# A fused attention and bilinear FFN kernel: regrouping the matmuls between batch 1's pairs, and a later kv for batch 2

The kernel runs on one core of one Trainium2 chip. The metric is device time in microseconds (us), the median of several executions. Engines in the profile: PE is TensorE (matmuls), PEld its weight loads, DVE is VectorE, ACT is ScalarE, POOL is GpSimd, SP issues transfers.

## The reference

```python
kv  = einsum('bhsd,bhse->bhde', k, v)            # 8 batches, 8 heads, 576 tokens, head size 64
out = einsum('bhsd,bhde->bhse', q, kv)
rms = sqrt(mean(out * out, axis=-1) + 1e-6)
x   = (out / rms * g_norm), heads side by side   # 4608 x 512
y   = ((x @ w_a) * (x @ w_b)) @ w_out            # 512 -> 1536 -> 512
```

## The kernel before

The FFN works in strips of 512 tokens. For each strip come the products with w_a and w_b for 12 slices of d_ff, and then four output groups of 128 tokens, each the sum of 12 products with w_out in one bank of PSUM, the memory that TensorE writes its sums to. One such product I call a unit. While strip 0's output groups run, the kernel also computes attention of batch 1, whose four pairs of heads are put between pieces of six units each. I call this part batch 1's stretch:

```python
A = Attn(1)
h1, h2 = range(0, FC // 2), range(FC // 2, FC)        # FC = 12
...
ffn_o(0, 0, X[0])                                     # output group 0, in bank 4
pieces = [(1, h1), (1, h2), (2, h1), (2, h2), (3, h1), (3, h2)]
for n, (g, fcs) in enumerate(pieces):
    halves[0] = n > 0          # from here a product is two matmuls of 64 columns
    o_mm(0, g, O, fcs)         # six units, all groups in bank O = 3
    if fcs is h2:
        o_out(0, g, O)         # copy the finished group out, and store it
    if 0 <= n - 2 < NP:        # NP = 4 pairs
        A.pss(n - 2, SS)       # sums of squares (PE), then rs (ACT)
        A.pst(n - 2, X[n % 2]) # xt = q kv * rs (DVE)
    if 0 <= n - 1 < NP:
        A.x(n - 1, X[(n - 1) % 2])    # q times kv (PE); X is banks 4,5 or 0,1
        A.psq(n - 1, X[(n - 1) % 2])  # its squares, sq (ACT)
    if n < NP:
        A.qtr(n, 2)            # transposes of q (PE), in bank 2
        A.kv1(n, 2)            # kv (PE), in the same bank
        A.kv_out(n, ...)       # kvb (ACT)
        A.qtr_out(n, 2)        # qT (DVE)
```

In the next strip a unit is another thing: one slice of d_ff with w_a and then with w_b. Batch 2's kv (40 matmuls, four pairs) stands there after unit `k0 = 5`, and its reader 1.5 units later, in the middle of unit 7. Numbers ending in .5 mean "between the w_a half and the w_b half of a unit". Batch 2's v comes in two loads, 512 KB and 64 KB; the second is "the last piece".

## Time and profile before

| | before |
|---|---|
| time, first three runs | 312.58 us (312.45 to 313.01) |
| span of the profiled run | 310.8 us |
| TensorE busy | 98% at granted clock 1.00 |
| waits of TensorE in batch 1's stretch | 0.58 us |
| wait in batch 2's kv | 0.24 us |

TensorE is nearly always busy and the ends of its matmuls are modelled, so its waits hardly show in the busy shares. They are read from the distances between starts, as the prediction does below. The lines themselves are shown there.

### The profile page before, as it was taken

How to read it: one execution, taken by the hardware profiler on the slowest of the kernel's cores; microseconds unless marked ns; L12 is line 12 of the kernel's file. 1: busy time of each engine (PE TensorE's matmuls, PEld its weight loads, DVE VectorE, ACT ScalarE, POOL GpSimd, SP SyncE). 2: the span in 40 equal slices, each digit the busy share in tenths (PEclk: the TensorE clock that was granted, in tenths of full speed). 3: DMA queues.
4: the chain of work that ended last, by engine and by line, in shares of the span. 5: the costliest groups of instructions: out<-in, count | busy, mean ns of one | idle time of the engine just before them, and what ended most of it. 6: DMA issues, size and time to landing. Idle time of an engine off the chain costs nothing.

```text
span 310.8 us, 6542 instructions
## 1 busy us (share of the span) xinstructions
PE 304.3 (98%) x2684; PEld 157.6 (51%) x2701; DVE 140.6 (45%) x235; ACT 117.0 (38%) x231; POOL 101.3 (33%) x123
## 2 busy tenths in 40 slices
PE   7899999999999999999999999999999999999996
PEld 3444476655555555555555555444444444444444
DVE  4544335458248603484386123752782143214321
ACT  3743255354255313551564034632651233123310
POOL 8954991093274630043646300221240000000000
PEclk9999999999999999999999999999999999999999
DMA  8999999999899999047998990073021200030002
GB/s 180 197 196 199 201 188 168 161 169 184 174 137 185 139 174 193 2 84 134 178 177 118 162 188 2 19 160 110 20 51 42 103 1 0 34 103 0 0 36 101
DMA packets 94403, 36.29 MB, mean 117 GB/s; under 512 B 64934, under 2 KB 89894, under 8 KB 94374
## 3 DMA queue, kind: packets, MB, share of 16 engines
q0 software_dynamic: 59120, 18.44, 56.6%
q1 hardware_dynamic: 34786, 16.93, 25.0%
q10 hardware_dynamic: 468, 0.51, 0.6%
q8 instruction: 21, 0.34, 0.5%
q14 instruction: 8, 0.07, 0.1%
HBM read 37.78 MB, written 12.98 MB: 163 GB/s over the span
## 4 chain that ended last, share of the span: by engine, by line
PE 79%; DMA 12%; POOL 7%; issue 1%; ACT 0%; POOLq 0%
PE P L161 77%; DMA wb_t<-in_moe_w_b_dram 6%; DMA vtl<-in_v_dram 4%; DMA wo_t<-in_moe_w_out_dram 2%; PE P L293 1%; PE P L178 1%; POOL vt L119 1%; POOL qt L119 1%; POOL qs L142 1%; POOL kt L119 1%; POOL wa_t L477 0%; POOL wb_t L477 0%; POOL wo_t L134 0%; POOL ktl L145 0%; POOL vtl L145 0%
## 5 line engine op out<-in xcount | busy, mean ns | idle before, releaser
L377 DVE TENSOR_TENSOR ab<-P,asb 128x512 bf16<-128x512 f32 x108 | 74.4, 691 | 103.2 <-PE P L161 99.9
L161 PE MATMUL P<-xt,wb_t 128*64 128x512 bf16 (+1 forms) x641 | 111.4, 379 | 0.2
L161 PE MATMUL P<-xt,wa_t 128*64 128x512 bf16 (+1 forms) x636 | 111.0, 379 | 0.6 <-issue 0.2
L373 ACT CAST asb<-P 128x512 bf16<-128x512 f32 x108 | 63.1, 586 | 89.6 <-PE P L161 89.5
L161 PE MATMUL P<-wo_t,ab 128*64 128x512 bf16 (+3 forms) x673 | 95.5, 371 | 0.3
L161 PEld LDWEIGHTS <-ab 128*64 128x64 bf16 (+1 forms) x678 | 47.5, 106 | 45.0
L161 PEld LDWEIGHTS <-wa_t 128*64 128x64 bf16 (+1 forms) x644 | 46.0, 106 | 46.2 <-issue 0.6
L161 PEld LDWEIGHTS <-wb_t 128*64 128x64 bf16 (+1 forms) x644 | 45.8, 106 | 45.8
L330 POOL TENSOR_TENSOR sqt<-rst,g_all 128x512 f32<-128x512 f32 (+1 forms) x24 | 25.0, 1046 | 83.0 <-ACT rst L323 83.0
L429 ACT COPY osb<-P 128x512 f32<-128x512 f32 x17 | 10.0, 586 | 70.2 <-PE P L161 60.2
L431 DVE COPY osb<-P 128x512 f32<-128x512 f32 x18 | 12.4, 691 | 44.9 <-PE P L161 40.4
L142 POOL DMA_DIRECT2D qs<-in_q_dram x12 | 19.8, 1654 | 0.7 <-issue 0.3
L314 DVE TENSOR_REDUCE sst<-sqt 128x8 f32<-128x512 f32 (+1 forms) x24 | 16.3, 680 | 1.7 <-ACT sqt L310 1.5
L339 DVE TENSOR_TENSOR qv<-P,sqt 128x512 bf16<-128x512 f32 x18 | 12.3, 681 | 0.0
L330 POOL TENSOR_TENSOR k_x<-rst,g_all 128x512 f32<-128x512 f32 x6 | 6.3, 1044 | 17.4 <-ACT rst L323 17.4
L323 ACT ACTIVATE rst<-sst,eps_t 128x8 f32<-128x8 f32 (+1 forms) x30 | 9.0, 300 | 7.2 <-DVE sst L314 7.0
L310 ACT ACTIVATE sqt<-P 128x512 f32<-128x512 f32 x18 | 10.5, 585 | 0.1
L243 DVE SCALAR_TENSOR_TENSOR xt<-P,g_col,rs 128x288 bf16<-128x288 f32 x16 | 7.5, 511 | 5.1 <-ACT rs L233 5.1
L134 POOL DMA_DIRECT2D wo_t<-in_moe_w_out_dram x12 | 6.4, 530 | 6.7 <-DMA wb_t<-in_moe_w_b_dram 3.2
L233 ACT ACTIVATE rs<-P,eps_t 128x576 f32<-128x576 f32 (+1 forms) x9 | 6.1, 689 | 3.7 <-PE P L161 3.4
L139 POOL COPY gate<-qT 1x1 bf16<-1x1 bf16 x5 | 0.9, 177 | 18.9 <-DVE kvs L618 14.0
L444 PE MATMUL P<-zeros 128*128 128x512 bf16 x16 | 5.8, 510 | 1.2 <-DVE eps_t L461 1.2
(72 smaller groups left out, 131.7 us busy)
## 6 DMA issues: line engine op xcount, KB each, us to landing
out_dram<-osb SPq DMA_DIRECT2D x23, 256.0 KB, 2.1
qs<-in_q_dram POOLq DMA_DIRECT2D x12, 288.0 KB, 7.5
ktl<-in_k_dram POOLq DMA_DIRECT2D x6, 512.0 KB, 9.6
vtl<-in_v_dram POOLq DMA_DIRECT2D x6, 512.0 KB, 12.2
out_dram<-osb SPq DMA_DIRECT2D x13, 128.0 KB, 2.4
wo_t<-in_moe_w_out_dram POOLq DMA_DIRECT2D x12, 128.0 KB, 6.0
wa_t<-in_moe_w_a_dram POOLq DMA_DIRECT2D x5, 256.0 KB, 8.9
wb_t<-in_moe_w_b_dram POOLq DMA_DIRECT2D x5, 256.0 KB, 9.5
```

What stands on the lines that cost most here:

```text
L119: nc.gpsimd.dma_start(out=t[:, hs, :, :], in_=src[b, hs].rearrange("h (t c) d -> t h c d", c=EC))
L142: nc.gpsimd.dma_start(out=d[:, hs, :], in_=q[b, hs].rearrange("h t d -> t h d"))
L161: nc.tensor.matmul(o[r], lhsT=lhsT[:, r], rhs=rhs, **kw)
L310: nc.scalar.activation(sqt[c % 3][r], self.by_head(c)[r], AF.Square)
L314: nc.vector.reduce_sum(sst[c % 3][r], sqt[c % 3][r].rearrange("t j p d -> t (j p) d"), axis=mybir.AxisListType.X,)
L323: nc.scalar.activation(rst[c % 3][r], sst[c % 3][r], AF.Abs_reciprocal_sqrt, bias=eps_t[r], scale=1.0 / D,)
L330: nc.gpsimd.tensor_mul(sqt[c % 3][r].rearrange("t j p d -> t (j p) d"), rst[c % 3][r].unsqueeze(2).to_broadcast([n, H, D]), g_all[r].unsqu ...
L339: nc.vector.tensor_mul(t[r].rearrange("t (p j) d -> t j p d", j=2), self.by_head(c)[r], sqt[c % 3][r])
L373: nc.scalar.copy(self.t, self.a)
L377: nc.vector.tensor_mul(abt[self.s % 2][self.fc], self.b, self.t)
L429: nc.scalar.copy(t, P[:, i, :])
L431: nc.vector.tensor_copy(t, P[:, i, :])
```

## The change

The intent: let group 1 finish early in its own bank (bank 1), so that group 2 can follow at once without waiting for the copy out. That frees the cut between pieces from the boundaries of groups, so that more units can stand in front of the first pairs, whose loads are late. Batch 2's kv also moves half a unit back, behind its load.

```diff
-    h1, h2 = range(0, FC // 2), range(FC // 2, FC)
...
-    pieces = [(1, h1), (1, h2), (2, h1), (2, h2), (3, h1), (3, h2)]
-    for n, (g, fcs) in enumerate(pieces):
+    cuts = (12, 20, 27, 33, 36, 42, 48)
+    for n, cut in enumerate(cuts[1:]):
         halves[0] = n > 0
-        o_mm(0, g, O, fcs)
-        if fcs is h2:
-            o_out(0, g, O)
+        for i in range(cuts[n], cut):
+            g, fc = divmod(i, FC)
+            bank = X[1] + 1 if g == 1 else O
+            o_mm(0, g, bank, (fc,))
+            if fc == FC - 1:
+                o_out(0, g, bank)
...
-        k0, x0 = {1: (5, 6.5), 2: (1, 2.5), ...
+        k0, x0 = {1: (5.5, 6.5), 2: (1, 2.5), ...
```

The pieces become 8, 7, 6, 3, 6, 6 units.

More of the change, by code (lines that the diff above doesn't have):

```diff
@@ L608, in slot @@
             xs = tuple(x0 + x for x in (0, 1.5, 2.5, 4, 5))
-        k0, x0 = {1: (5, 6.5), 2: (1, 2.5), 3: (4, 5.5), 4: (0, 0.5), 5: (4, 5.5), 6: (0, 0.5)}[s]
+        k0, x0 = {1: (5.5, 6.5), 2: (1, 2.5), 3: (4, 5.5), 4: (0, 0.5), 5: (4, 5.5), 6: (0, 0.5)}[s]
         if n == k0 and s in (1, 2, 3, 5):
```

## The prediction

> **What bounds the kernel now.** I read the page first: busy shares, then the chain that ended last.
>
> ```profile
> PE 304.3 (98%) x2684; PEld 157.6 (51%) x2701; DVE 140.6 (45%) x235; ACT 117.0 (38%) x231; POOL 101.3 (33%) x123
> ...
> PE 79%; DMA 12%; POOL 7%; issue 1%; ACT 0%; POOLq 0%
> ```
>
> TensorE is the bound: busy for 98% of the span at granted clock 1.00 in every slice, and the chain is its matmuls from 60 us to the end. Both kernels do the same matmuls; only their order changes, apart from two units that run 128 columns wide and no longer as two 64-column halves. So the change can only win or lose the short holes between TensorE's instructions. The ends of matmuls are modelled, so I read holes from the distance between starts. The timeline of TensorE, asked in narrow windows over batch 1's stretch (start, us, group), gives:
>
> ```profile
> 39.13 0.45 PE L202 MATMUL P<-ident,qt 96*64 96x96 bf16 x12
> 39.60 0.38 PE L178 MATMUL P<-vt,kt 96*64 96x64 bf16 x12
> ...
> 41.33 0.45 PE L202 MATMUL P<-ident,qt 96*64 96x96 bf16 x12
> 41.82 0.38 PE L178 MATMUL P<-vt,kt 96*64 96x64 bf16 x12
> ...
> 43.31 0.44 PE L161 MATMUL P<-sq,ones 128*64 128x288 bf16 x4
> 43.55 0.44 PE L161 MATMUL P<-qT,kvb 128*64 128x288 bf16 x4
> 43.80 0.45 PE L202 MATMUL P<-ident,qt 96*64 96x96 bf16 x12
> 44.05 0.38 PE L178 MATMUL P<-vt,kt 96*64 96x64 bf16 x12
> ...
> 45.54 0.44 PE L161 MATMUL P<-sq,ones 128*64 128x288 bf16 x4
> 45.92 0.44 PE L161 MATMUL P<-qT,kvb 128*64 128x288 bf16 x4
> 46.16 0.45 PE L202 MATMUL P<-ident,qt 96*64 96x96 bf16 x12
> 46.42 0.38 PE L178 MATMUL P<-vt,kt 96*64 96x64 bf16 x12
> ```
>
> These are, pair by pair, the transposes of q (L202), kv (L178), the sums of squares (sq,ones) and q times kv (qT,kvb). Without a wait, transposes to kv is 0.26 us (46.16 to 46.42), squares to q times kv 0.24 (43.31 to 43.55). So kv of pair 0 waited 0.47 - 0.26 = 0.21, kv of pair 1 waited 0.49 - 0.26 = 0.23, and q times kv of pair 2 waited 0.38 - 0.24 = 0.14: together 0.58 us. What released them: the v loads are issued at 34.24, 36.47, 38.37 and 40.59 us in the GpSimd timeline, and the view of tile vt, one window for each, gives 5.3, 5.3, 5.6 and 5.6 us to landing, so they land at 39.54, 41.8, 43.97 and 46.19. The first two are the two waits for kv: batch 1's loads come one pair every 2.2 us, and TensorE keeps pace with them. The third wait is another thing; ScalarE and VectorE in that window:
>
> ```profile
> 43.78 0.74 ACT L233 ACTIVATE rs<-P,eps_t 128x576 f32<-128x576 f32 x1 [1.01 <-PE P L161]
> 44.42 0.64 ACT L225 ACTIVATE sq<-P 128x576 bf16<-128x576 f32 x1
> 44.95 0.43 ACT L189 CAST kvb<-P 64x64 bf16<-64x64 f32 x2
> 44.56 0.94 DVE L243 SCALAR_TENSOR_TENSOR xt<-P,g_col,rs 128x288 bf16<-128x288 f32 x2 [1.30 <-ACT rs L233]
> 45.42 0.45 DVE L209 COPY qT<-P 128x576 bf16<-128x576 bf16 x1
> ```
>
> A chain of latencies: squares of pair 0 (43.31) -> rs (43.78) -> sq of pair 1 and the cast of kvb on ScalarE, two xt products on VectorE -> qT of pair 2 (45.42 to 45.87) -> q times kv of pair 2 at 45.92. The two branches end within 0.05 us of each other.
>
> The fourth hole is kv of batch 2, where the chain of waits leaves the loads and joins TensorE:
>
> ```profile
> 47.20 13.45 DMA vtl<-in_v_dram
> 60.65 0.04 issue
> 60.69 0.69 PE P L178 x32
> ```
>
> The timeline has all 40 of these matmuls starting at 60.32 and the next unit at 61.19, 0.87 us; the same 40 take 0.63 us in the chain of waits at 86.37. So 0.24 us is waited for the last piece of v.
>
> **What the Trainium skill says.** "Perfetto Trace Analysis", section "Tensor Engine Instruction (MATMUL, LD_WEIGHTS)": a matmul's reported start comes after its semaphores are satisfied, and its end is estimated. The trace agrees: the waits show as late starts while busy stays at 98%. "TensorEngine Tiling (Array Packing)", "Key Properties": changing the tiling mode drains the engine. The trace agrees: from the last 128-column unit at 38.82 (39.13 less 0.31, single starts) to the first transpose is 0.31 us against 0.216 from unit to unit, 0.09 more; both kernels have this once in this stretch. "PSUM — Partial Sum Buffer", "PSUM bank collisions raise a hardware error": two engines must not use one bank at once, hence group 2 may start in the bank of group 1 only after its copy out. That is why the change needs a second bank. The trace of before shows no wait of group 2 for the copy: kv of pair 1 starts at 41.82 and the first unit at 42.01, the usual 0.19.
>
> **The change, part by part.** A unit (one fc of an output group, two 64-column matmuls) is 0.216 us. Before, pieces of 6, 6, 6, 6, 6, 6 units stood between pairs; after, 8, 7, 6, 3, 6, 6. Instruction order on VectorE and ScalarE is unchanged (the two listings differ in line numbers alone), and GpSimd's loads do not depend on this, so the landings stay. Replaying with the distances above:
> - Group 0 starts at 35.15 and takes 12 x 0.216, to 37.74. Eight units (1.73) and the mode change (0.09): transposes at 39.56, kv of pair 0 at 39.82. It landed at 39.54: no wait. Against 39.60 before, +0.22 (two units, 0.43, less the wait of 0.21).
> - kv 0.19, seven units 1.51, q times kv 0.24, transposes 0.26: kv of pair 1 at 42.02, landed 41.8, no wait. +0.20.
> - kv 0.19, six units 1.29: squares of pair 0 at 43.50, +0.19 (43.31). q times kv 43.75, transposes 43.99, kv of pair 2 at 44.25 (landed 43.97).
> - kv 0.19, three units 0.65: TensorE could do the squares of pair 1 at 45.09. But sq of pair 1 hangs on rs of pair 0, and that on the squares of pair 0, which are 0.19 later: sq starts at 44.61, ends 45.25, squares at about 45.31. A wait of 0.22. Then q times kv of pair 2 could start at 45.55, but qT of pair 2 comes 0.19 later than before: 45.92 + 0.19 = 46.11. A wait of 0.56.
> - Transposes, then kv of pair 3 at 46.61 against 46.42: +0.19. Its load landed at 46.19 and is not waited for in either kernel.
> - From there 6 and 6 units as before, everything shifted alike. Group 3 returns to group 2's bank: that copy starts after qT at about 45.99, takes 0.68, done by 46.7, and TensorE comes at 46.80. No wait.
>
> So 0.44 us of waits for loads and 0.14 for the chain go, and 0.78 of waits for the same chain come: about +0.19 at the end of the stretch. The gain was eaten because the units moved forward were the ones that covered the chain.
> - kv of batch 2 half a unit later: half a unit is four pairs, 0.86 us. It starts at 60.32 + 0.19 + 0.86 = 61.4, and the last piece landed at 60.65. The wait of 0.24 goes. Its reader is one unit (1.73 us) on, and the cast takes 0.42: nothing new waits.
>
> Sum: +0.19 - 0.24 = -0.05 us. All after 61 us is TensorE back to back, so this reaches the end: 312.58 - 0.05 = 312.53, call it 312.5.
>
> **Rivals.** (1) All four holes vanish, as the intent must be: -0.58 - 0.24 = -0.8, 311.8 us. Against it: kv of pair 3 cannot start before its load at 46.19 plus about 0.06 (39.54 to 39.60), so at most 46.42 - 46.25 = 0.17 of the 0.58 can be won while the loads land as they do. With the second hole that is -0.4, 312.2, the best I can see. It would come about if the chain has slack that the trace hides. (2) The three-unit piece costs more: the squares of pair 1 come late, so rs, sq and qT of pair 3 queue up behind one another, and a second wait follows at q times kv of pair 3 or at group 3's bank. In my replay each has 0.1 to 0.3 us to spare; if both were lost, +0.3, 312.8. (3) kv in the middle of a unit delays ScalarE or VectorE there: both idle over 1 us before each unit's copy in the timeline, so I give it nothing.
>
> **Range and chances.** All of this is under 0.3% of the time, and three runs of before already differ by 0.56 us. I take 312.1 (rival 1's floor, and a little) to 312.95 (rival 2, and the scatter). Over 2% either way would be 6 us, ten times every hole together: 1% each.
>
> **What would show it.** In the profile after: kv of pairs 0 and 1 about 0.26 us after their transposes; over 0.5 us from squares to q times kv in pair 2 (0.8 expected, 0.38 before); kv of pair 3 near 46.6; 40 matmuls of batch 2's kv in 0.63 us from about 61.4. The prediction is wrong if kv of pair 3 starts before 46.4, if v's landings move by more than 0.2 us, or if a hole over 0.2 us stands after 47 us that before does not have.

## The result

| | before | after |
|---|---|---|
| median of six runs | 312.69 us (312.36 to 313.13) | 312.86 us (312.66 to 313.05) |
| ratio | | 1.0004, 95% interval 0.9992 to 1.0017 |
| span of the profiled run | 310.8 us | 311.1 us |
| group 0's first unit to the last copy, same profiles | 272.71 us | 272.68 us |

A ratio is the mean time of one kernel's fast runs over that of the other's of the same rounds, so it is not quite the ratio of the medians. The medians differ by 0.17 us, less than either scatters.

The last row is the measure that I use from here on: the distance from the start of group 0's first unit to the start of the last copy on ScalarE, both single starts in the trace. It leaves out the kernel's first 35 us, which neither the change nor any experiment touches and which scatter. From the first matmul to group 0 took 33.96 us in the profile of before, 34.32 in that of after, and 33.96 to 34.44 over all thirteen profiles. That scatter alone is larger than the effect sought.

The distance is not wholly free of those 35 us, since group 0's start moves against batch 1's loads. In before, before_2 and kv_only, which wait for these loads, v of pair 0 landed 38.37 to 38.40 us after the first matmul and the squares of pair 3 stood at 48.52 to 48.56, though group 0 started anywhere from 33.96 to 34.14. A kernel that waits for the loads thus makes good a later start of group 0, and its distance comes out shorter; the changed kernel does not (squares of pair 3 at 48.74 to 49.18 in the five profiles with its pieces and both banks).

The page of the changed kernel, busy shares and the chain that ended last:

```profile
PE 304.7 (98%) x2682; PEld 157.0 (50%) x2699; DVE 140.8 (45%) x235; ACT 117.3 (38%) x231; POOL 101.3 (33%) x123
...
PE 97%; ACT 1%; DVE 1%; issue 1%
```

The loads are gone from the chain (they were 12% of it before, and the issues on POOL 7%). That alone does not show that no load is waited for: cuts_only below has the same shares, and its kv waited 0.22 us for a load. The landings show it for this profile: v of pairs 0 to 3 landed at 4.02, 6.24, 8.46 and 10.65 us after group 0's first unit and kv started at 4.69, 6.89, 9.12 and 11.47. Of the 1% each of ACT and DVE, 0.75 and 0.93 us stand in batch 1's stretch, and most of the rest before group 0. The timeline of TensorE shows the stretch (start, us, group). To compare with before, subtract group 0's first unit: 35.51 us here, 35.15 before.

```profile
39.92 0.45 PE L202 MATMUL P<-ident,qt 96*64 96x96 bf16 x12
40.20 0.35 PE L178 MATMUL P<-vt,kt 96*64 96x64 bf16 x12
...
42.15 0.42 PE L202 MATMUL P<-ident,qt 96*64 96x96 bf16 x12
42.41 0.35 PE L178 MATMUL P<-vt,kt 96*64 96x64 bf16 x12
...
43.89 0.41 PE L161 MATMUL P<-sq,ones 128*64 128x288 bf16 x4
...
44.83 0.82 PE L161 MATMUL P<-wo_t,ab 128*64 128x512 bf16 x6
45.68 0.44 PE L161 MATMUL P<-sq,ones 128*64 128x288 bf16 x4
46.49 0.44 PE L161 MATMUL P<-qT,kvb 128*64 128x288 bf16 x4 [0.37 <-DVE qT L209]
46.73 0.45 PE L202 MATMUL P<-ident,qt 96*64 96x96 bf16 x12
46.99 0.38 PE L178 MATMUL P<-vt,kt 96*64 96x64 bf16 x12
```

The kv of pairs 0 and 1 now follow their transposes after 0.28 and 0.26 us (0.47 and 0.49 before): the waits for the loads are gone. The three units at 44.83 end at about 45.48, but the squares of pair 1 start at 45.68, a wait of 0.20. From there to q times kv of pair 2 is 0.81 us instead of 0.24, a wait of 0.57, and the profile names its releaser: the copy of qT on VectorE. ScalarE and VectorE of the changed kernel in that window:

```profile
44.34 0.74 ACT L233 ACTIVATE rs<-P,eps_t 128x576 f32<-128x576 f32 x1 [1.02 <-PE P L161]
44.98 0.64 ACT L225 ACTIVATE sq<-P 128x576 bf16<-128x576 f32 x1
45.52 0.43 ACT L189 CAST kvb<-P 64x64 bf16<-64x64 f32 x2
45.12 0.94 DVE L243 SCALAR_TENSOR_TENSOR xt<-P,g_col,rs 128x288 bf16<-128x288 f32 x2 [1.30 <-ACT rs L233]
45.98 0.46 DVE L209 COPY qT<-P 128x576 bf16<-128x576 bf16 x1
```

It is the same chain with the same lengths: from the squares of pair 0 to q times kv of pair 2 it is 46.49 - 43.89 = 2.60 us, and before 45.92 - 43.31 = 2.61. Only fewer units lie over it now. Batch 2's kv in the changed kernel:

```profile
61.75 0.82 PE L178 MATMUL P<-vtl,ktl 128*64 128x64 bf16 x40
62.38 0.60 PE L161 MATMUL P<-xt,wb_t 128*64 128x512 bf16 x3
```

The 40 matmuls take 0.63 us to the next unit, and took 0.87 before: that wait is gone.

### The profile page after: what moved, and what is told of

Its sections match the earlier page's. It is cut to its first block, busy times and chain, and to the rows that moved or that the text cites. A ratio compares the mean times of both kernels' runs of the same rounds, so it can differ in the third digit from the quotient of the medians.

```text
span 311.1 us, 6538 instructions
## 1 busy us (share of the span) xinstructions
PE 304.7 (98%) x2682; PEld 157.0 (50%) x2699; DVE 140.8 (45%) x235; ACT 117.3 (38%) x231; POOL 101.3 (33%) x123
## 4 chain that ended last, share of the span: by engine, by line
PE 97%; ACT 1%; DVE 1%; issue 1%
PE P L161 90%; PE P L444 2%; PE P L178 1%; PE P L293 1%; PE P L202 1%; PE P L216 0%; DVE xt L243 0%; ACT sq L225 0%; ACT rs L233 0%; PE P L501 0%; DVE qT L209 0%; PE P L505 0%; PE P L517 0%; DVE zeros L455 0%; ACT o_end L668 0%
## 5 line engine op out<-in xcount | busy, mean ns | idle before, releaser
L444 PE MATMUL P<-zeros 128*128 128x512 bf16 x16 | 6.7, 573 | 1.2 <-DVE eps_t L461 1.2
```

What stands on the lines that cost most here:

```text
L444: nc.tensor.matmul(P[:, i, 0:cols], lhsT=zeros[:, 0:128], rhs=zeros[:, 0:cols], start=True, stop=True)
```

## The experiments

Theory A is that of the prediction: the waits for loads go, the wait for the chain takes their place, and the later kv wins a wait back. Rivals are named run by run. The measure is the distance defined above: 272.71 us before, 272.68 after. Each distance is from one profile. cuts_2, before_2, after_2 and the three held runs were executed once; their granted clock was 0.998 to 1.00.

### kv_only: the second part of the change alone

```diff
-        k0, x0 = {1: (5, 6.5), ...
+        k0, x0 = {1: (5.5, 6.5), ...
```

> The kernel before with the second part of the change alone (kv of batch 2 half a unit later). Theory A (waits come back): batch 1's stretch is as before, kv of batch 2 starts 0.86 us later than before and its 40 matmuls take 0.63 us and not 0.87, so the distance from group 0's first unit to the last copy out of the kernel (272.72 us before, 272.68 after) is 272.48, 0.24 less than before; time 0.999 of before. Rival B (the second part is worth nothing, a later wait for the same landing takes its place): 272.7.

Measured: distance 272.36, kv at 25.92 us after group 0's first unit, its 40 matmuls in 0.63 us; time 312.52 us against 312.57, ratio 0.9996 (0.9983 to 1.0008), not told apart from before. The wait in batch 2's kv is gone and no later one replaces it. But this profile does not show that the move did it: the last piece landed at 24.69, and kv at its old place, 25.06, would not have waited either. after_2 below shows it. A further 0.11 is from the start of group 0: v of pair 0 landed at 4.30 and not 4.41 after it, so the stretch, which is bound by the loads, ended 0.11 earlier. The loads themselves had hardly moved (38.40 us after the first matmul, 38.37 before); group 0 had started 0.14 later.

### cuts_only and cuts_2: the first part alone, looked at twice

```diff
-        k0, x0 = {1: (5.5, 6.5), ...      # from the changed kernel
+        k0, x0 = {1: (5, 6.5), ...
```

> The changed kernel without its second part. Theory A: the stretch of batch 1 ends 0.2 us later than before (kv of pair 3 and all after it), and the wait of batch 2's kv for its last piece shrinks by just that, from 0.24 to about 0.05, as the landing stays: distance from group 0's first unit to the last copy 272.72 to 272.77, as before, time ratio 1.000. Rival B: the second part is worth nothing, so this equals the changed kernel, 272.68, with no wait in kv of batch 2. Rival C: the two parts add up, so 272.72 + 0.2 = 272.92.

Measured: distance 272.89, ratio 1.0002 (0.9990 to 1.0014). That is rival C's figure and not theory A's. The stretch did end 0.20 later than before (squares of pair 3 at 14.76 us, before 14.56), but the wait in kv stayed at 0.22 us, because the last piece of v landed 0.19 later too. I had taken the landing as fixed. So I looked at the same kernel again, and at before.

> The changed kernel without its second part, profiled once more. In the first look batch 2's kv still waited 0.22 us, as its last piece landed 0.19 later than in the profile of before. Theory A (scatter of the landing): kv of batch 2 starts again 25.36 us after group 0's first unit; it waits max(0, landing - 25.49 + 0.04) and the distance is 272.67 plus that wait. Rival B: again a landing near 25.7 and a distance of 272.89.

The timeline of the first look, then that of the second:

```profile
60.81 1.05 PE L178 MATMUL P<-vtl,ktl 128*64 128x64 bf16 x40
61.66 0.41 PE L161 MATMUL P<-xt,wa_t 128*64 128x512 bf16 x2
```

```profile
60.53 0.82 PE L178 MATMUL P<-vtl,ktl 128*64 128x64 bf16 x40
61.16 0.63 PE L161 MATMUL P<-xt,wa_t 128*64 128x512 bf16 x4
```

The 40 matmuls took 0.85 us in one look and 0.63 in the other, with no instruction changed: the landing was at 25.68 us after group 0's first unit and at 23.65. Without the wait the distance was 272.67, as theory A had it. Over the thirteen profiles this landing lies between 23.65 and 25.68. So the three figures told nothing about how the two parts combine, only where the piece landed: the parts add up when it lands late, and the second part is worth nothing when it lands early.

### before_2 and after_2: both kernels once more

> The kernel before, profiled once more, to see how far the landing of batch 2's last piece of v moves from run to run: 25.49 us after group 0's first unit in the first profile, 24.2 to 25.7 in the five others. Theory A (the landing scatters by itself, with no regard to the kernel): it may land anywhere from 24.2 to 25.7, and kv of batch 2 waits only where it lands after about 25.3; distance 272.45 to 272.8, the stretch of batch 1 alike. Rival B (an early kv makes the landing late): again at 25.4 or later, wait again 0.24.

The stretch repeated: squares of pair 3 at 14.42 us (14.56 in the first profile), the landing was 25.42, and kv waited 0.31. Here theory A and rival B cannot be told apart, but cuts_2 (an early kv, and the earliest landing of all) speaks against B, and so does after_2 below (a later kv, and a landing at 25.58). These two show that kv's place does not fix the landing. Whether it shifts the odds stays open: of four profiles with kv at the early place three had a landing at 25.42 to 25.68, of nine with the later kv only after_2. The distance was 272.87, larger than I had allowed, and a wait elsewhere did it.

> The changed kernel once more. It waits for no load between group 0 and the end, so the distance should repeat to 0.03 us, 272.68, wherever the last piece of v lands, while the start of group 0 after the first matmul may lie anywhere from 33.9 to 34.5 us.

The stretch repeated exactly (squares of pair 3 at 14.76 against 14.77), and batch 2's kv waited for nothing although the piece landed at 25.58, which an undelayed kv at 25.36 would have met. It is the one profile that shows the second part of the change at work. But the distance was 272.96 and not 272.68. The timeline of after_2 at the start of strip 2, then that of after:

```profile
81.69 1.25 PE L161 MATMUL P<-wo_t,ab 128*64 128x512 bf16 x10
83.03 0.84 PE L161 MATMUL P<-xt,wa_t 128*64 128x512 bf16 x6
```

```profile
82.00 1.25 PE L161 MATMUL P<-wo_t,ab 128*64 128x512 bf16 x10
83.07 0.81 PE L161 MATMUL P<-xt,wa_t 128*64 128x512 bf16 x6
```

Ten 64-column matmuls are five units, 1.08 us; strip 2's first unit comes after 1.07 in one and after 1.34 in the other. This unit reads x of batch 2, which a transfer transposes; the third of these landed 47.68 us after group 0 in after_2 and 46.64 in after, and the unit started at 47.81. It waited so in two of thirteen profiles, once for each kernel (0.26 and 0.20 us). So my claim that the changed kernel waits for no load up to the end was too strong: this wait is there now and then, for both.

### even_cuts: pieces of 7, 7, 5, 5, 6, 6

```diff
-    cuts = (12, 20, 27, 33, 36, 42, 48)
+    cuts = (12, 19, 26, 31, 36, 42, 48)
```

> The changed kernel with pieces of 7, 7, 5, 5, 6, 6 units and not 8, 7, 6, 3, 6, 6: the chain from the squares of pair 0 to q times kv of pair 2 starts earlier and has more units over it. Theory A: no wait at kv of pairs 0 and 1, about 0.16 at kv of pair 2, about 0.2 at q times kv of pair 2 (0.56 in the changed kernel), none at the squares of pair 1; kv of pair 3 lies against its load, about 0.17 earlier than in the kernel before; the distance from group 0's first unit to the last copy is 272.72 - 0.19 - 0.24 = 272.3, ratio 0.9986 of before. Rival B (what costs is not the chain but the second bank or the early group 2): no better than the changed kernel, 272.68.

Measured: distance 272.35 (272.3 expected), 312.44 us against 312.57, ratio 0.9994 (0.9982 to 1.0006). With five units over the chain and not three, squares of pair 1 to q times kv of pair 2 is 0.38 us and not 0.81, so 0.14 of wait; kv of pair 2 waited for its load, as expected. The second bank and the early group 2 are as in the changed kernel, so rival B falls.

### squares_early: the head of the chain three units earlier

```diff
         for i in range(cuts[n], cut):
+            if n == 2 and i == cuts[n] + 3:
+                A.pss(0, SS)
+                A.pst(0, X[0])
...
-        if 0 <= n - 2 < NP:
+        if 0 < n - 2 < NP:
```

> The changed kernel, pieces unchanged, with the squares of pair 0 and their products (pss and pst of pair 0) put three units earlier, in the middle of their piece. Theory A (the chain that starts at the squares of pair 0 holds q times kv of pair 2): the wait at the squares of pair 1 goes (0.2), that at q times kv of pair 2 shrinks from 0.56 to at most 0.4, kv of pair 3 comes 0.3 to 0.37 us earlier and lies against its load; distance from group 0's first unit to the last copy about 272.3. Rival B (the copy of qT of pair 2 waits for its own kv alone, three units are too few whatever the squares do): q times kv of pair 2 stays where it is, distance 272.68.

Measured: distance 272.30 (272.3 expected), 312.41 us, ratio 0.9994 (0.9982 to 1.0007). The timeline of TensorE in this kernel, from the squares of pair 0 to kv of pair 3 (group 0's first unit is at 35.64):

```profile
43.37 0.41 PE L161 MATMUL P<-sq,ones 128*64 128x288 bf16 x4
...
45.60 0.41 PE L161 MATMUL P<-sq,ones 128*64 128x288 bf16 x4
46.23 0.44 PE L161 MATMUL P<-qT,kvb 128*64 128x288 bf16 x4 [0.22 <-DVE qT L209]
46.73 0.38 PE L178 MATMUL P<-vt,kt 96*64 96x64 bf16 x12
```

No unit was moved, only the squares of pair 0 with what follows them (rs, xt). The wait at the squares of pair 1 went, squares to q times kv of pair 2 fell from 0.81 to 0.63, and kv of pair 3 came at 46.73 - 35.64 = 11.09 us after group 0 and not at 11.48. The chain that begins at the squares of pair 0 is thus shown to hold pair 2. It is not alone: the squares came 0.65 us earlier and q times kv of pair 2 only 0.38, and 0.39 of its wait stayed. In this profile sq of pair 1 waits 0.15 for TensorE and qT of pair 2 waits 0.18 for the cast of kvb, so a second chain (q times kv of pair 1, sq, kvb, qT) stands close behind, and rival B has that much right. kv of pair 3 did not lie against its load, as I had expected: that landed at 10.77.

### one_bank: the changed pieces without the second bank

```diff
-            bank = X[1] + 1 if g == 1 else O
+            bank = O
```

> The changed kernel with group 1 back in group 2's bank, pieces as changed. Group 2's first unit now follows group 1's last at once and must wait for the copy out of the bank. Theory A: about 0.25 from the last unit to the copy's start, 0.59 of the copy and 0.05, so a wait of about 0.85 us inside the second piece (0.22 would be the usual distance, so about 0.65 to 0.7 of hole); nothing later makes it good, since the stretch waits for no load: distance from group 0's first unit to the last copy 272.68 + 0.65 = 273.3 to 273.4, ratio 1.002. Rival B (the second bank is only a convenience, the wait is given back by the waits at pair 2): 272.7 to 272.9.

Measured: distance 273.54, 313.51 us against 312.54, ratio 1.003 (1.0013 to 1.0047): slower by 0.3%, clear of the scatter. The timeline of TensorE in this kernel:

```profile
40.31 0.81 PE L161 MATMUL P<-wo_t,ab 128*64 128x512 bf16 x6
41.80 0.84 PE L161 MATMUL P<-wo_t,ab 128*64 128x512 bf16 x6 [0.68 <-ACT osb L429]
```

Group 2's first unit waits for the copy out of group 1's bank, and q times kv of pair 0, three units behind it, comes 0.84 us later than in the changed kernel (7.23 and 6.39 after group 0). I had expected 0.65 to 0.7, having taken off the usual distance between units from a sum that did not contain it. Nothing later made it good. So the second bank is not a nicety: without it these pieces lose 0.84 us.

### held_before, held_after and held_bank: batch 1 without its loads

```diff
-                kk, vv, rows = kt[self.b], vt[self.b], [EP] * EC
+                kk, vv, rows = kt[0], vt[0], [EP] * EC       # batch 0's k and v, long there
...
-                        qt[self.b][:, 2 * p + j, c, :],
+                        qt[0][:, 2 * max(p, 1) + j, c, :],   # and its q; k and v likewise
```

Batch 1's result is wrong. Its loads still run, so the transfers are as they were.

> Pieces as in the kernel before, batch 2's kv half a unit later, and batch 1 computed from batch 0's q, k and v that are already there (pairs 1, 1, 2, 3; a wrong result on purpose for batch 1), so that nothing in the stretch hangs on batch 1's loads, which still run. Theory A (the waits at kv of pairs 0 and 1 are the loads): both go, all after them comes 0.44 us earlier; the wait of about 0.14 at q times kv of pair 2 stays, since it is the chain. Distance from group 0's first unit to the last copy 272.71 - 0.44 - 0.24 = 272.03, or 272.1 if the kv of batch 2 now meets its landing. Rival B (those two waits are the return of bank 2 or the tiling mode, not the loads): 272.4 as in the run with batch 2's kv alone.

Measured: 272.20, where theory A said 272.03 to 272.1 and rival B 272.4. The waits at kv of pairs 0 and 1 went, but 0.16 us came up that I had not foreseen.

> The same edit on the changed kernel. Theory A: the changed kernel waits for no load in this stretch, only for the chain, so nothing moves: q times kv of pair 2 at 10.97 us after group 0's first unit, distance 272.68. Rival B (its pairs also hang on loads): earlier by what the loads cost, up to 0.4.

Measured: 272.67, and q times kv of pair 2 at 10.97: not moved by 0.01 us. The changed kernel's stretch hangs on no load.

> Pieces of six as in the kernel before, batch 2's kv later, batch 1 computed from batch 0's loads (wrong on purpose), and group 1 in its own bank. In the same kernel without the bank (held_before, 272.20) the first unit of group 2 came 0.35 us after kv of pair 1 and not 0.19. Theory A (with the loads gone the next wait is group 2's, for the copy out of group 1's bank): that 0.16 goes, distance 272.04. Rival B (something else stood there): 272.2.

Measured: 272.03 (272.04 expected). This kernel is held_before with group 1 in its own bank. The two timelines, held_before first:

```profile
41.56 0.35 PE L179 MATMUL P<-vt,kt 96*64 96x64 bf16 x12
41.91 0.41 PE L161 MATMUL P<-wo_t,ab 128*64 128x512 bf16 x2
```

```profile
41.69 0.35 PE L179 MATMUL P<-vt,kt 96*64 96x64 bf16 x12
41.87 0.60 PE L161 MATMUL P<-wo_t,ab 128*64 128x512 bf16 x4
```

From kv of pair 1 to group 2's first unit is 0.35 us with one bank and 0.18 with two. In the kernel before, then, the wait for the bank stood hidden behind the wait for v of pair 1: had the loads come earlier, TensorE would have waited for the bank instead.

## Why the prediction was right

The time (312.86 inside 312.1 to 312.95) and the mechanism held. Against group 0's first unit, the steps came out so:

| step | predicted | measured |
|---|---|---|
| kv of pair 0, change of start | +0.22 | +0.24 |
| kv of pair 1 | +0.20 | +0.22 |
| squares of pair 0 | +0.19 | +0.22 |
| wait at the squares of pair 1 | 0.22 | 0.20 |
| wait at q times kv of pair 2 | 0.56 | 0.57 |
| kv of pair 3 | +0.19 | +0.21 |
| wait in kv of batch 2 | -0.24 | -0.24 |
| to the end | -0.05 | -0.04 |

That close an agreement owes something to luck. The stretch after is rigid: the squares of pair 3 stand at 14.76 or 14.77 us after group 0 in all five profiles with these pieces (after, after_2, cuts_only, cuts_2, held_after). The stretch before rides on its loads: 14.56, 14.42 and 14.45 in three profiles (before, before_2, kv_only); the later group 0 starts, the smaller it is. So the first part of the change costs 0.2 to 0.35 us there, and my 0.19 is the low end of it, because group 0's start in the profile that I used (33.96) is the earliest of all thirteen. The second part wins 0 to 0.3, depending on where the last piece of v lands. That -0.24 was measured for it is luck too: in the profile of after the piece landed at 24.20, so kv would have waited for nothing at its old place either. By the same landing one of the prediction's own signs of being wrong came up, that v's landings move by more than 0.2 us: this piece moved from 25.49 to 24.20.

- That the chain from the squares of pair 0 holds q times kv of pair 2 was argued; squares_early shows it.
- That the two waits at kv were the loads was read from landings; held_before and held_bank show it. They also bear out the argument against rival 1: with the loads out of the way and group 1 in its own bank, but not with the loads, the distance falls by 0.68 us, to 272.03, which is near rival 1's 0.8; the chain's wait of about 0.14 makes the rest.
- "The trace of before shows no wait of group 2 for the copy" was right, but the bank would have been next, by 0.16 us.
- The step that failed, without harm to the sum, is "so the landings stay". It held for batch 1's loads in absolute time (v of pair 3 at about 46.2 in both profiles) but not for batch 2's last piece, which landed over 2 us apart in two looks at one kernel. In the changed kernel kv stands behind the latest landing seen (25.68).
- "All after 61 us is TensorE back to back" was too much by a wait of 0.2 to 0.26 us at strip 2's start, in two of thirteen profiles.
- The measured median lies 0.36 us above my figure. Of that, 0.11 is my starting point, the first three runs of before (312.58; all six gave 312.69). The rest is within the scatter. A later start of group 0, which costs the changed kernel more than the one before, would do it, but where group 0 started in the runs without a profile is not known.

even_cuts and squares_early have shorter distances than both kernels (272.35 and 272.30 us), but so has kv_only (272.36), and none is told from before by its timed runs. The bound that the prediction works out under rival 1, about 0.4 us or 0.13%, is what squares_early reached (0.41), with a late group 0 (34.44 us after the first matmul) and with kv of pair 3 still 0.32 behind its load. What more there is to win was not tried. Open is why the kernel's start scatters, and why the transposes of x come late now and then.

## What to carry to other kernels

Work that is moved forward to cover one wait is taken away from another place: before moving it, follow each chain that the work lay over (here squares, rs, xt, the copy of qT) and count whether enough is left over it. When a gain is below the scatter of whole runs, measure a distance inside the trace that leaves out what the change doesn't touch, check whether its own starting point moves against the loads, look at the same kernel twice, and put a consumer behind the latest landing seen rather than behind the one of a single profile.

## What the Trainium skill lacked or had wrong

- "TensorE: Matmul & The Clock Gate", section "Back-to-back issue gap", gives about 131 ns per matmul as the sustained spacing for N = 512 in a stream of weight loads and matmuls, and about 216 ns for the isolated one. In this stream of weight loads and matmuls the spacing was 0.216 us for a 128-column matmul, and the same for two of 64 columns side by side. The measurement agrees with the page's isolated figure, not with the sustained one.
- "TensorEngine Tiling (Array Packing)", section "Key Properties", says that a change of tiling mode drains the engine, without a size. Here the change from 128-column units to the 64-column transposes took 0.309 us from start to start against 0.216, so 0.09 (0.309 or 0.310 in all thirteen profiles). No run parts the change of mode from the change of shape.
- "PSUM — Partial Sum Buffer", section "PSUM bank collisions raise a hardware error", has the rule but not what the hand-over of a bank costs. A group that follows another at once in the same bank came 0.84 us later than in a bank of its own, with a copy of 0.59 us between them.
- "DMA: Bandwidth & Descriptors" gives no figure for the scatter of a landing between runs of one kernel. The same 64 KB piece, issued behind the same loads, took 13.85 us from issue to landing in one look and 11.69 in another.
